# One sum, one inverse, one product a group: where the attention weights of batch 0 are divided

## The chip, the cores and the metric

The kernel runs on one core of a Trainium2 chip. The metric is device time in microseconds (us) of one execution. The core has five engines with programs of their own: TensorE (PE in the profile, with its weight loads as PEld), VectorE (DVE), ScalarE (ACT), GpSimd (POOL) and SyncE (SP, which here issues nearly all DMAs). Each engine runs its instructions in the order of its program and waits at semaphores for the others.

## The reference

Attention of 2 batches with 8 heads, 576 positions and 64 values a head, in which scores more than tau under the row's maximum are dropped; then two mixtures of dense layers over the 1152 tokens.

```
scores = scale * (q @ k^T)
scores = where(scores >= max(scores) - tau, scores, -1e9)
attn = exp(scores - max(scores))
attn = attn / (sum(attn) + 1e-9)
x = attn @ v                       # 1152 tokens x 512
h = max(x @ w1, x @ w2, x @ w3);  y = h @ w_out
out = sum over 4 experts e of p[:, e] * (relu(y @ m_w1[e]) @ m_w2[e])
```

## The kernel before

Every fp32 operand of a product is split in two parts of type fp32r, "hi" (the rounded value) and "lo" (the rest), and three or four products of parts make one. So nearly everything that TensorE reads was first copied once and subtracted once by ACT, DVE or POOL.

**Stages.** Stage A (`attention_fast`, L466) is the attention of batch 0 and has the core for itself. Stage B is the attention of batch 1, laid between the products of the dense layers of the first 512 tokens; then follow the dense layers of the other 640 tokens. The products (L832) can begin when stage A has delivered X, its result.

**Stage A.** Heads are taken in four pairs (jobs). A pair has two groups of queries and nine steps: a step is one tile of 128 queries of one head against 576 keys, and one step in nine holds the last 64 queries of both heads (`st.h is None`). A step runs through: `qk` (scores, PE, L301), `peak` (row maximum, DVE, L312), `power` (exp, ACT, L319), `limit` and `weigh` (DVE, L315 and L324: drops weights below the threshold and sums the row into `st_sum`), `norm` (L327), `turn` (transposes on PE, L342 and L345), `cut_hi` and `cut_lo` (split of the turned weights into `am`, for keys 0 to 511, and `ar`, for the last 64 keys). The big split goes by turns through PE and ACT (mode "pe") or through a copy `tcopy` and POOL (mode "pool"). When a group's steps are done, `gather` multiplies with the values (L418), adds the two halves of the product (L421 on ACT, L423 on DVE) and splits the sum into X (L432 on ACT, L435 on POOL).

`norm` divides the weights by their sum before they are turned: two instructions on one element a row on DVE, then a pass over 576 elements on POOL (on DVE for the last two steps):

```
nc.vector.tensor_scalar(out=su, in0=su, scalar1=1e-9, ..., op0=ALU.add)
nc.vector.reciprocal(out=re, in_=su)
last = (nc.vector if swift else nc.gpsimd).tensor_scalar(out=em, in0=em, scalar1=re, scalar2=even, op0=ALU.mult, op1=ALU.add)
```

`even` is 0 unless tau is negative; then all weights are dropped and every one becomes 1/576.

**Order.** In stage A the framework's scheduler orders each engine's instructions from the order in which the code issues them; from the dense layers on, the code's own order stands. In stage A step i is weighed while step i-1 is divided and turned and step i-2 is split. Buffers: scores, turned weights and all else in PSUM have two tiles each (`S`, `T`, `U`). Stage B calls the same `norm` and is otherwise not touched.

## Time and profile before

| what | before |
|---|---|
| time, median of 3 runs | 746.56 us (745.12 to 747.57) |
| the profiled execution's own time | 749.09 us |
| its span, first to last instruction | 747.3 us |
| PE, PEld busy over the span | 715.7, 636.4 us (96%, 85%) |
| DVE, ACT, POOL busy over the span | 378.3, 339.0, 392.4 us (51%, 45%, 53%) |
| mean granted TensorE clock | 0.988 |

The last 1.8 us of the own time lie around the span. A busy share over the whole span is a mean over stages that are limited by different things, so the rows below split the span.

### The profile page before, as it was taken

The page shows a single profiled execution, that of the slowest core. Times are in us where ns is not written, and L with a number is a line of the kernel's source. Part 1 is how long each engine was busy: PE and PEld are TensorE (multiplying, and loading weights), DVE is VectorE, ACT ScalarE, POOL GpSimd, SP SyncE. Part 2 cuts the span into 40 slices and gives each one's busy share as a digit, 9 for nine tenths or more (in the row PEclk, how much of TensorE's full clock was granted, in tenths as well). Part 3 has the DMA queues.
Part 4 walks back from the last instruction along what each step waited for, and adds up shares of the span by engine and source line. Part 5 has one row for each costly group of instructions (what it writes and reads, how often), then busy time and mean ns, then how long its engine had stood idle before and what let it go on. Part 6 is the DMA issues. An engine that isn't in the chain of part 4 may idle for free.

```text
span 747.3 us, 11716 instructions
## 1 busy us (share of the span) xinstructions
PE 715.7 (96%) x4103; PEld 636.4 (85%) x4103; DVE 378.3 (51%) x900; ACT 339.0 (45%) x716; POOL 392.4 (53%) x435
## 2 busy tenths in 40 slices
PE   4798999999899999999999999999999999999997
PEld 3787889777688788888888899999998998998996
DVE  6798988775265765766766421112222222222222
ACT  5688984444544655465454412333321321321320
POOL 5789785777554555564564524544623522522520
PEclk9799999999999999999999999999999999999999
DMA  6702006876724124122322233223412313312303
GB/s 183 227 22 49 1 1 187 261 226 204 199 78 113 59 73 122 57 73 57 86 61 66 71 113 85 68 58 91 132 50 85 99 43 85 104 45 77 113 2 71
DMA packets 89369, 71.01 MB, mean 95 GB/s; under 512 B 24158, under 2 KB 75358, under 8 KB 89310
## 3 DMA queue, kind: packets, MB, share of 16 engines
q1 hardware_dynamic: 88860, 69.96, 32.7%
q8 instruction: 33, 0.54, 0.3%
q10 hardware_dynamic: 418, 0.30, 0.2%
q14 instruction: 26, 0.21, 0.1%
q0 software_dynamic: 32, 0.00, 0.0%
HBM read 61.59 MB, written 8.65 MB: 94 GB/s over the span
## 4 chain that ended last, share of the span: by engine, by line
PE 77%; DVE 5%; ACT 5%; POOL 5%; issue 3%; DMA 3%; SPq 1%; POOLq 0%; ACTq 0%; DVEq 0%
PE ps L832 63%; PE u L418 5%; PE s L301 4%; PE t L342 3%; POOL a L630 2%; DVE st_negm L312 1%; DMA vrem<-in_v_dram 1%; ACT em L319 1%; DMA words<-in_moe_w_dram 1%; POOL b L656 1%; PE u L175 1%; DMA krem<-in_k_dram 1%; DVE raw L664 1%; ACT a L626 1%; PE t L388 1%
## 5 line engine op out<-in xcount | busy, mean ns | idle before, releaser
L630 POOL TENSOR_TENSOR a<-raw,a 128x512 fp32r<-128x512 f32 (+1 forms) x116 | 145.1, 1256 | 163.6 <-ACT a L626 160.3
L832 PE MATMUL ps<-b,hh 128*128 128x512 f32 x576 | 184.3, 393 | 0.0
L832 PEld LDWEIGHTS ps<-b,hh 128*128 128x128 f32 x576 | 107.3, 188 | 20.4
L782 ACT ACTIVATE hh<-ps 128x320 fp32r<-128x320 f32 (+1 forms) x96 | 46.8, 488 | 152.3 <-PE ps L832 151.9
L832 PE MATMUL ps<-b,hl 128*128 128x512 f32 x288 | 113.1, 393 | 0.0
L832 PE MATMUL ps<-y1h,a 128*128 128x320 f32 x512 | 112.8, 309 | 0.0
L630 POOL TENSOR_TENSOR b<-raw,b 128x512 fp32r<-128x512 f32 x64 | 82.8, 1296 | 53.4 <-ACT b L626 53.4
L785 DVE SCALAR_TENSOR_TENSOR hl<-ps,hh 128x320 fp32r<-128x320 f32 (+1 forms) x96 | 53.4, 556 | 108.9 <-ACT hh L782 108.8
L626 ACT ACTIVATE a<-raw 128x512 fp32r<-128x512 f32 (+1 forms) x116 | 69.4, 612 | 58.8 <-PE ps L832 19.1
L801 DVE SCALAR_TENSOR_TENSOR acc<-ps,pr,acc 128x512 f32<-128x512 f32 x63 | 47.2, 749 | 80.4 <-PE ps L832 80.3
L832 PE MATMUL ps<-y0h,a 128*128 128x512 f32 x256 | 85.1, 403 | 0.8 <-POOL a L630 0.8
L832 PEld LDWEIGHTS ps<-y1h,a 128*128 128x128 f32 x512 | 85.4, 188 | 0.3
L319 ACT ACTIVATE em<-s,st_negm 128x576 f32<-128x576 f32 x72 | 53.3, 744 | 70.9 <-DVE st_negm L312 70.7
L332 POOL TENSOR_SCALAR em<-em,st_r,even 128x576 f32<-128x576 f32 x70 | 57.5, 824 | 43.2 <-DVE st_r L331 41.6
L832 PE MATMUL ps<-y1l,a 128*128 128x320 f32 x256 | 79.1, 309 | 0.0
L312 DVE TENSOR_REDUCE st_negm<-s 128x1 f32<-128x576 f32 x72 | 54.1, 753 | 48.9 <-PE s L301 48.4
L301 PE MATMUL s<-K,QS 128*128 128x288 f32 x320 | 59.7, 315 | 6.4 <-DVE em L324 3.2
L832 PE MATMUL ps<-x1h,a 128*128 128x320 f32 x288 | 63.4, 309 | 0.0
L324 DVE SCALAR_TENSOR_TENSOR em<-s,st_thr,em 128x576 f32<-128x576 f32 x72 | 58.2, 812 | 9.9 <-ACT em L319 7.8
L832 PEld LDWEIGHTS ps<-b,hl 128*128 128x128 f32 x288 | 54.1, 188 | 10.0
L301 PEld LDWEIGHTS s<-K,QS 128*128 128x128 f32 x320 | 49.8, 197 | 11.3 <-issue 6.0
L832 PEld LDWEIGHTS ps<-y0h,a 128*128 128x128 f32 x256 | 47.8, 191 | 9.6 <-POOL a L630 1.2
(129 smaller groups left out, 1271.1 us busy)
## 6 DMA issues: line engine op xcount, KB each, us to landing
raw<-in_moe_w_dram SPq DMA_DIRECT2D x128, 256.0 KB
words<-in_moe_w_dram SPq DMA_DIRECT2D x18, 512.0 KB
kept_w<-raw SPq DMA_DIRECT2D x18, 256.0 KB
raw<-kept_w SPq DMA_DIRECT2D x18, 256.0 KB
kraw<-in_k_dram SPq DMA_DIRECT2D x30, 128.0 KB
words<-in_moe_w_out_dram SPq DMA_DIRECT2D x8, 384.0 KB
vraw<-in_v_dram SPq DMA_DIRECT2D x8, 256.0 KB
qraw<-in_q_dram SPq DMA_DIRECT2D x7, 256.0 KB
```

The costliest lines, as they stand in the source:

```text
L301: nc.tensor.matmul(st.s[:, kh, 0:HS], lhsT=l, rhs=r, start=i == 0, stop=i == len(terms) - 1)
L312: nc.vector.tensor_reduce(out=st.stat["negm"], in_=views(st)[0], op=ALU.max, axis=AX.XY, negate=True)
L319: nc.scalar.activation(out=ev, in_=sv, func=AF.Exp, bias=st.stat["negm"])
L324: nc.vector.scalar_tensor_tensor(out=ev, in0=sv, scalar=st.stat["thr"], in1=ev, op0=ALU.is_ge, op1=ALU.mult, accum_out=st.stat["sum"])
L332: last = (nc.vector if swift else nc.gpsimd).tensor_scalar(out=em, in0=em, scalar1=re, scalar2=even, op0=ALU.mult, op1=ALU.add)
L418: at["valued"] = nc.tensor.matmul(pv, lhsT=l, rhs=r, start=i == 0, stop=i == len(terms) - 1)
L626: nc.scalar.activation(out=b["hi"], in_=b["raw"], func=AF.Copy)
L630: nc.gpsimd.tensor_tensor(out=b["lo"], in0=b["raw"], in1=f32(b["hi"]), op=ALU.subtract)
L782: nc.scalar.activation(out=hs[f][0][:, a:z], in_=ps, func=AF.Relu)
L785: nc.vector.scalar_tensor_tensor(out=hs[f][1][:, a:z], in0=ps, scalar=0.0, in1=f32(hs[f][0][:, a:z]), op0=ALU.max, op1=ALU.subtract)
L801: nc.vector.scalar_tensor_tensor(out=accs[t], in0=ps, scalar=pe, in1=accs[t], op0=ALU.mult, op1=ALU.add)
L832: nc.tensor.matmul(ps, lhsT=l, rhs=r, start=i == 0, stop=i == count - 1)
```

## The change

For batch 0 the weights go undivided through the transposes, the split and the product with the values. `weigh` writes the sum of a step into its column of a tile `sums` of the group. When a group's last step is weighed, `invert` adds 1e-9 to the 4 or 5 sums and inverts them in one instruction each, and copies each over 64 columns into `inv`. In `gather` PE turns `inv` (2 or 3 transposes into a tile `rt`), so that the inverses stand along the queries as X does, and DVE multiplies X with them. Around this: a step is turned and split one step after it was weighed (before: split two steps after). The split of `ar` moves from DVE to POOL, by way of a copy `arcopy` that ACT makes. The copy of the values to "hi" moves from ACT to POOL. A negative tau is now handled by scores of 0 (`qscale` is 0 then, a scale read from a tile) in place of `even`.

```
 def weigh(st):
-    nc.vector.scalar_tensor_tensor(
+    return nc.vector.scalar_tensor_tensor(
         out=ev, in0=sv, scalar=st.stat["thr"], in1=ev, op0=ALU.is_ge, op1=ALU.mult, accum_out=st.stat["sum"])
-def norm(st, swift=False):
+def norm(st):
...
-    last = (nc.vector if swift else nc.gpsimd).tensor_scalar(out=em, in0=em, scalar1=re, scalar2=even, op0=ALU.mult, op1=ALU.add)
+    nc.gpsimd.tensor_scalar(out=em, in0=em, scalar1=re, scalar2=1.0, op0=ALU.mult, op1=ALU.mult)
+    twice(st)
...
+def invert(grp):
+    n = 5 if grp.n > grp.nn else 4
+    su = grp.sums[:, 0:n]
+    nc.vector.tensor_scalar(out=su, in0=su, scalar1=1e-9, scalar2=None, op0=ALU.add)
+    nc.vector.reciprocal(out=su, in_=su)
+    flats = grp.inv.rearrange("p c h d -> p (c h) d")
+    nc.vector.tensor_copy(out=flats[:, 0:4], in_=su[:, 0:4, None].to_broadcast([P, 4, D]))
+    if n == 5:
+        nc.vector.tensor_copy(out=flats[:, 4:6], in_=su[:, 4:5, None].to_broadcast([P, 2, D]))
...
 # values
-    nc.scalar.activation(out=V[:, :, :, 0:D], in_=vn, func=AF.Copy)
+    if job.b == 0:
+        nc.gpsimd.tensor_scalar(out=V[:, :, :, 0:D], in0=vn, scalar1=1.0, scalar2=1.0, op0=ALU.mult, op1=ALU.mult)
...
 # cut_hi
-        nc.scalar.activation(out=grp.ar[0][r, cols], in_=st.tm[r, r], func=AF.Copy)
+        if ar_pool:
+            if r.start == 0:
+                st.arcopy = atile([P, P], F32, "arcopy")
+            nc.scalar.activation(out=st.arcopy[r, r], in_=st.tm[r, r], func=AF.Copy)
...
 # cut_lo
-        nc.vector.tensor_tensor(out=grp.ar[1][r, cols], in0=st.tm[r, r], in1=f32(grp.ar[0][r, cols]), op=ALU.subtract)
+        if hasattr(st, "arcopy"):
+            hi, lo = (x[r, cols] for x in grp.ar)
+            nc.gpsimd.tensor_scalar(out=hi, in0=st.arcopy[r, r], scalar1=1.0, scalar2=1.0, op0=ALU.mult, op1=ALU.mult)
+            nc.gpsimd.tensor_tensor(out=lo, in0=st.arcopy[r, r], in1=f32(hi), op=ALU.subtract)
...
 # gather
+    if grp.job.b == 0:
+        rt = ptile_at("U", [P, 3 * P])
+        for x in range(3 if n > grp.nn else 2):
+            nc.tensor.transpose(rt[:, x * P:(x + 1) * P], grp.inv[:, x].rearrange("p h d -> p (h d)"), ident)
+        parts = [(slice(0, P), slice(0, grp.nn), slice(0, grp.nn))]
+        if n > grp.nn:
+            parts += [(slice(h * D, (h + 1) * D), slice(grp.nn, n), slice(grp.nn + h * REM, grp.nn + (h + 1) * REM)) for h in range(2)]
+        for r, c, rc in parts:
+            nc.vector.tensor_tensor(out=x32[r, c], in0=rt[r, rc], in1=x32[r, c], op=ALU.mult)
+        yield
...
 # attention_fast
-    for i in range(n + 3):
+    for i in range(n + 1):
-        old = steps[i - 2] if 0 <= i - 2 < n else None
+        old = steps[i - 1] if i else None
...
+            if st:
+                at["weighed"] = weigh(st)
+                twice(st)
+                if st.last:
+                    invert(st.grp)
...
-bufs_a = {"K1": 2, "K2": 2, "QS": 2, "V": 2, "VR": 2, "em": 3, "am": 6, "ar": 4}
+bufs_a = {"sums": 2, "inv": 1, "K1": 2, "K2": 2, "QS": 2, "V": 2, "VR": 2, "em": 3, "am": 6, "ar": 3}
```

The changed file has other line numbers; in it `qk` is L305, `peak` L322, `limit` L325, `power` L329, `weigh` L334, `invert` L355 to L360, `turn` L367 and L370, the copies of `ar` L407 to L433, the products with the values L453, the sum of halves L458, the turn of `inv` L464 and the new product L469.

On VectorE, in the middle of stage A, these ten instructions stood in a row (`st_sum` and `st_r` are a step's sum and its inverse, `u` the PSUM tile that holds the turned last keys):

```order
L324 SCALAR_TENSOR_TENSOR em,st_sum<-s,st_thr,em 128x576
L315 TENSOR_SCALAR st_thr<-st_negm,ntau 128x1
L400 TENSOR_TENSOR ar<-u,ar 128x128
L330 TENSOR_SCALAR st_sum<-st_sum 128x1
L331 RECIPROCAL st_r<-st_sum 128x1
L324 SCALAR_TENSOR_TENSOR em,st_sum<-s,st_thr,em 128x576
L312 TENSOR_REDUCE st_negm<-s 128x1
L330 TENSOR_SCALAR st_sum<-st_sum 128x1
L315 TENSOR_SCALAR st_thr<-st_negm,ntau 128x1
L331 RECIPROCAL st_r<-st_sum 128x1
```

and now, where a group ends (here the first pair's second group is inverted and its first group's result `x_407` is multiplied):

```order
L356 RECIPROCAL sums<-sums 128x5
L458 TENSOR_TENSOR x_407<-u,pvlo 64x256
L325 TENSOR_SCALAR st_thr<-st_negm,ntau 128x1
L334 SCALAR_TENSOR_TENSOR em,sums<-s,st_thr,em 128x576
L358 COPY inv<-sums 128x256
L360 COPY inv<-sums 128x128
L469 TENSOR_TENSOR x_407<-u,x_407 128x256
L334 SCALAR_TENSOR_TENSOR em,sums<-s,st_thr,em 128x576
L322 TENSOR_REDUCE st_negm<-s 128x1
L325 TENSOR_SCALAR st_thr<-st_negm,ntau 128x1
L322 TENSOR_REDUCE st_negm<-s 128x1
L334 SCALAR_TENSOR_TENSOR em,sums<-s,st_thr,em 128x576
```

The two small instructions of each step and the subtraction for `ar` have left; once a group an inverse, one or two copies and a product have come.

On TensorE, the first group's products with the values stood together, each head's product of `ar` right behind those of `am`:

```order
L342 MATMUL t<-ident,em 128x128 x4
L418 MATMUL u<-am,V 128x256 x4
L418 MATMUL u<-ar,VR 128x256
L418 MATMUL u<-am,V 128x256 x4
L418 MATMUL u<-ar,VR 128x256
L345 MATMUL u<-ident,em 128x128
```

and now the products of `ar`, whose operand comes from POOL, stand behind other work:

```order
L367 MATMUL t<-ident,em 128x128 x4
L453 MATMUL u<-am,V 128x256 x4
L305 MATMUL s<-K_132,QS 128x288
L305 MATMUL s<-K_133,QS 128x288
L305 MATMUL s<-K_132,QS 128x288
L305 MATMUL s<-K_133,QS 128x288
L176 MATMUL u<-ident,QN 128x128 x4
L418 MATMUL t<-ident,em 128x128 x4
L425 MATMUL t<-am,nident 128x512
L453 MATMUL u<-ar,VR 128x256
L453 MATMUL u<-am,V 128x256 x4
```

Between the first four products and the one of `ar` there are now 13 matmuls of other steps.

On ScalarE, at the start of stage A, four steps' exponentials (`em<-s`) stood ahead of the copies of pair 1's values (`V`, `VR`), which wait for DMAs; of them these two, from one row on:

```order
L319 ACTIVATE em<-s,st_negm 128x576 x2
L626 ACTIVATE a<-raw 128x512
L646 ACTIVATE b<-words 128x512
L246 ACTIVATE V<-vraw 128x8x64
L252 ACTIVATE VR<-vrem 64x64 x2
L319 ACTIVATE em<-s,st_negm 128x576
L375 ACTIVATE am<-t 128x4x128
```

and now three do, and the split of step 0 (`am`, `arcopy`) has come ahead of `VR`:

```order
L329 ACTIVATE em<-s,st_negm 128x576
L666 ACTIVATE a<-raw 128x512
L400 ACTIVATE am<-t 128x4x128
L407 ACTIVATE arcopy<-u 128x128
L666 ACTIVATE a<-raw 128x512
L686 ACTIVATE b<-words 128x512
L256 ACTIVATE VR<-vrem 64x64 x2
L426 ACTIVATE am<-t 128x4x128
L329 ACTIVATE em<-s,st_negm 128x576
```

The copy `V` has gone to POOL, and the fourth exponential stands behind `VR`. On SP the load of pair 1's values, `vraw`, has moved behind four of the five loads of `pr` and pair 2's `qraw`.

## Rows read from the trace of the kernel before

**Rows 1.** Windows: busy us and count per engine, then granted clock, DMA share, GB/s.

```profile
0.00:29.40 29.40, 15.31 (x61) 12.76 (x62) 18.80 (x53) 16.61 (x34) 16.74 (x32) 0.77 0.72 208
29.40:106.80 77.40, 72.12 (x542) 66.16 (x540) 70.38 (x233) 68.49 (x153) 66.82 (x95) 1.00 0.15 38
106.80:114.00 7.20, 6.55 (x47) 5.89 (x45) 5.87 (x16) 4.36 (x12) 3.18 (x5) 1.00 0.00 0
114.00:747.30 633.30, 621.67 (x3460) 551.61 (x3458) 283.23 (x601) 249.56 (x518) 305.66 (x305) 1.00 0.34 98
```

**Rows 2.** Groups by line and shape on DVE, 30 to 114 us: busy us, mean ns.

```profile
L324 DVE SCALAR_TENSOR_TENSOR em<-s,st_thr,em 128x576 f32<-128x576 f32 x31 | 24.9, 812 | 2.3 <-ACT em L319 1.5 <-issue 0.4
...
L331 DVE RECIPROCAL st_r<-st_sum 128x1 f32<-128x1 f32 x32 | 4.8, 155 | 0.3
L400 DVE TENSOR_TENSOR ar<-u,ar 128x128 fp32r<-128x128 f32 x16 | 4.4, 278 | 0.0
L330 DVE TENSOR_SCALAR st_sum<-st_sum 128x1 f32<-128x1 f32 x31 | 4.4, 146 | 0.3
...
L398 DVE TENSOR_TENSOR am<-t,am 128x256 fp32r<-128x256 f32 x8 | 3.1, 412 | 0.0
...
L400 DVE TENSOR_TENSOR ar<-u,ar 64x64 fp32r<-64x64 f32 x8 | 1.7, 219 | 0.1
```

**Rows 3.** Timeline of DVE: start us, duration us, instruction.

```profile
71.98 0.14 DVE L330 TENSOR_SCALAR st_sum<-st_sum 128x1 f32<-128x1 f32 x1
72.05 0.81 DVE L324 SCALAR_TENSOR_TENSOR em<-s,st_thr,em 128x576 f32<-128x576 f32 x1
...
74.50 0.28 DVE L400 TENSOR_TENSOR ar<-u,ar 128x128 fp32r<-128x128 f32 x1
74.70 0.75 DVE L312 TENSOR_REDUCE st_negm<-s 128x1 f32<-128x576 f32 x1
```

**Rows 4.** Groups by line and shape on POOL, 30 to 114 us.

```profile
L332 POOL TENSOR_SCALAR em<-em,st_r,even 128x576 f32<-128x576 f32 x31 | 25.4, 824 | 3.6 <-DVE st_r L331 2.2 <-DVE st_sum L330 0.7 <-PE u L175 0.4
...
L392 POOL TENSOR_SCALAR am<-tcopy 128x512 fp32r<-128x512 f32 x15 | 9.6, 637 | 2.8 <-ACT tcopy L372 2.7
L435 POOL TENSOR_TENSOR x0l<-x,x0h 128x256 fp32r<-128x256 f32 x7 | 5.1, 732 | 3.2 <-ACT x0h L432 3.1
...
L195 POOL TENSOR_SCALAR K<-K 128x64 fp32r<-128x64 f32 x6 | 1.4, 241 | 0.0
...
L435 POOL TENSOR_TENSOR x1l<-x,x1h 128x64 fp32r<-128x64 f32 x3 | 1.0, 320 | 0.0
```

**Rows 5.** Timeline of DVE at the start.

```profile
3.58 0.29 DVE L206 COPY kraw<-kraw 128x256 f32<-128x256 f32 x1 [0.29 <-DMA kraw<-in_k_dram]
...
5.11 0.15 DVE L898 TENSOR_SCALAR neg<-tau_c 128x1 f32<-128x1 f32 x1 [1.23 <-DMA tau_c<-in_tau_dram]
```

**Rows 6.** Timeline of PE: two runs of four transposes.

```profile
98.35 0.60 PE L342 MATMUL t<-ident,em 128*128 128x128 f32 x4
98.78 0.60 PE L388 MATMUL t<-ident,em 128*128 128x128 f32 x4
```

**Rows 7.** Waits of PE's weight loads, 30 to 114 us: total us, times, longest.

```profile
PEld u L418 <- DVE ar L400: 1.8, 2, 1.5
...
PEld t L342 <- POOL em L332: 0.9, 1, 0.9
```

**Rows 8.** Timeline at the end of stage A.

```profile
106.78 0.82 DVE L324 SCALAR_TENSOR_TENSOR em<-s,st_thr,em 128x576 f32<-128x576 f32 x1
...
108.47 0.58 DVE L332 TENSOR_SCALAR em<-em,st_r,even 128x576 f32<-128x576 f32 x1
...
110.40 0.60 PE L342 MATMUL t<-ident,em 128*128 128x128 f32 x4
```

**Rows 9.** Timeline of ACT at the start of stage A.

```profile
25.96 0.63 ACT L246 ACTIVATE V<-vraw 128x512 fp32r<-128x512 f32 x1 [1.55 <-DMA vraw<-in_v_dram]
...
27.56 0.74 ACT L319 ACTIVATE em<-s,st_negm 128x576 f32<-128x576 f32 x1
```

More of the change, by code (lines that the diff above doesn't have):

```diff
@@ L91, in fused_kernel @@
     nc.gpsimd.dma_start(out=tau_c, in_=tau.rearrange("(a o) -> a o", o=1).to_broadcast([P, 1]))
+    qscale = cst.tile([P, 1], F32, name="qscale")
     def xy_tiles(g, nm):
@@ L177, in prep @@
             qo = (0, W + 2 * REM)[h]
-            nc.scalar.activation(out=QS[:, qo:qo + MAIN], in_=tq, func=AF.Copy, scale=SCALE)
+            nc.scalar.activation(out=QS[:, qo:qo + MAIN], in_=tq, func=AF.Copy, scale=qscale)
             yield
@@ L189, in prep @@
             nc.scalar.activation(out=k1r, in_=trk, func=AF.Copy)
-            nc.scalar.activation(out=q1r, in_=trq, func=AF.Copy, scale=SCALE)
+            nc.scalar.activation(out=q1r, in_=trq, func=AF.Copy, scale=qscale)
             yield
@@ L219, in head @@
             nc.scalar.activation(out=d1, in_=tk, func=AF.Copy)
-            nc.scalar.activation(out=QS[:, qo:qo + MAIN], in_=tq, func=AF.Copy, scale=SCALE)
+            nc.scalar.activation(out=QS[:, qo:qo + MAIN], in_=tq, func=AF.Copy, scale=qscale)
             nc.vector.tensor_tensor(out=K2[:, ko:ko + MAIN], in0=tk, in1=f32(d1), op=ALU.subtract)
@@ L234, in prep_first @@
         head(1)
-        nc.scalar.activation(out=q1r, in_=trq, func=AF.Copy, scale=SCALE)
+        nc.scalar.activation(out=q1r, in_=trq, func=AF.Copy, scale=qscale)
         for t in (K1, K2):
@@ L245, in values @@
         vn = vt[:, :, :, 0, :]
-        nc.scalar.activation(out=V[:, :, :, 0:D], in_=vn, func=AF.Copy)
+        if job.b == 0:
+            nc.gpsimd.tensor_scalar(out=V[:, :, :, 0:D], in0=vn, scalar1=1.0, scalar2=1.0, op0=ALU.mult, op1=ALU.mult)
+        else:
+            nc.scalar.activation(out=V[:, :, :, 0:D], in_=vn, func=AF.Copy)
         nc.gpsimd.memset(f32(VR), 0.0)
@@ L310, in peak @@
         st.col = (st.h or 0) * S
-        st.stat = {x: atile([P, 1], F32, f"st_{x}") for x in ("negm", "thr", "sum", "r")}
+        st.stat = {x: atile([P, 1], F32, f"st_{x}") for x in ("negm", "thr", "sum", "r") if st.grp.job.b or x in ("negm", "thr")}
+        if not st.grp.job.b:
+            if not hasattr(st.grp, "sums"):
+                st.grp.sums, st.grp.inv = atile([P, 5], F32, "sums"), atile([P, 3, 2, D], F32, "inv")
+            col = 4 if st.h is None else 2 * st.ci + st.h
+            st.stat["sum"] = st.grp.sums[:, col:col + 1]
         nc.vector.tensor_reduce(out=st.stat["negm"], in_=views(st)[0], op=ALU.max, axis=AX.XY, negate=True)
@@ L378, in cut_hi @@
                 grp.ar = [atile([P, grp.n], F32R, "ar") for _ in "hl"]
-            nc.scalar.activation(out=grp.ar[0][r, cols], in_=st.tm[r, r], func=AF.Copy)
+            if ar_pool:
+                if r.start == 0:
+                    st.arcopy = atile([P, P], F32, "arcopy")
+                nc.scalar.activation(out=st.arcopy[r, r], in_=st.tm[r, r], func=AF.Copy)
+            else:
+                nc.scalar.activation(out=grp.ar[0][r, cols], in_=st.tm[r, r], func=AF.Copy)
     def cut_lo(st):
@@ L497, in attention_fast @@
                 peak(st)
-            if 0 <= i - 1 < n - 1:
-                norm(steps[i - 1], i - 1 >= n - SWIFT)
             if nxt:
@@ L504, in attention_fast @@
                 qk(nxt)
-            if st and not nxt:
-                power(st)
-                limit(st)
-                weigh(st)
-                at["normed"] = norm(st, True)
-                turn(steps[i - 1])
-                urgent.enter_context(tc.issue_after(at["normed"].ins))
             if old:
-                cut_hi(old, next(modes) if old.h is not None and i - 2 < n - CALM else "dve")
+                at["turned"] = turn(old)
             advance()
-            if nxt:
+            if st:
                 power(st)
             if old:
-                cut_lo(old)
-            if nxt:
+                cut_hi(old, next(modes) if old.h is not None and i - 1 < n - CALM else "dve", i - 1 < n - CALM)
+            if st:
                 limit(st)
             advance()
-            if nxt:
-                weigh(st)
-                if i:
-                    turn(steps[i - 1])
-            if st and not nxt:
-                at["turned"] = turn(st)
+            if old:
+                cut_lo(old)
+            if st:
+                at["weighed"] = weigh(st)
+                twice(st)
+                if st.last:
+                    invert(st.grp)
             if old:
@@ L895, in fused_kernel @@
     stage = open_attention("A", {"S": 2, "T": 2, "U": 2}, bufs_a)
-    neg = cst.tile([P, 1], F32, name="neg")
-    nc.vector.tensor_scalar(out=neg, in0=tau_c, scalar1=0.0, scalar2=None, op0=ALU.is_lt)
-    even = cst.tile([P, 1], F32, name="even")
-    nc.vector.tensor_scalar(out=even, in0=neg, scalar1=1.0 / S, scalar2=None, op0=ALU.mult)
+    nc.vector.tensor_scalar(out=qscale, in0=tau_c, scalar1=0.0, scalar2=SCALE, op0=ALU.is_ge, op1=ALU.mult)
     ntau = cst.tile([P, 1], F32, name="ntau")
-    nc.vector.scalar_tensor_tensor(out=ntau, in0=neg, scalar=3e38, in1=tau_c, op0=ALU.mult, op1=ALU.subtract)
+    nc.vector.tensor_scalar(out=ntau, in0=tau_c, scalar1=0.0, scalar2=-1.0, op0=ALU.max, op1=ALU.mult)
     for _ in attention_fast(first, cycle(MODES_A)):
```

11 lines of the change are left out of this document (7 added, 4 removed).

## The prediction

> **What bounds the kernel now.** I read the windows first, cut where the work changes [rows 1]. Behind 114 us stand the dense layers and batch 1's attention, and PE is busy for 621.67 of 633.30 us there: that part starts when stage A ends and takes what it takes. The change touches it in one place only, a constant in batch 1's division on POOL, which is at half load there. So what it is worth is read from the 114 us before. The first 29.4 us run at a mean granted clock of 0.77 (a part of them at 1.2 GHz) with the DMA engines 72% busy; they are ruled by what has landed. From 29.4 to 106.8 us the clock is 1.00 (2.4 GHz), the DMA share is 0.15, and the reader is to see that no engine is far behind another: PE 72.12 of 77.4 us (93%), its weight loads 66.16 (85%), DVE 70.38 (91%), ACT 68.49 (88%), POOL 66.82 (86%). In the last 7.2 us the tail runs out and PE begins to fill itself with products of the dense layers.
>
> Then the waits. PE's are few and short: of those in the list, 1.8 us fall to the split of `ar` on DVE and 0.9 us to the division on POOL [rows 7]. The exponentials are waited for by L324 for 1.5 us in all [rows 2]. With so little waiting, the length of the stage is mostly what the fullest engine has to do, so I count what each gets and loses. Which engine is the fullest is the first thing to choose: by matmul time it is PE, by weight loads it is DVE. Matmul durations overlap: two runs of four transposes are shown with 0.60 us each but start 0.43 us apart [rows 6], so PE can take more than its 93% seem to allow. I take DVE.
>
> The Trainium skill says the same in Perfetto Trace Analysis, Identifying the Most-Contended Engine: TensorE's matmul busy share is no good measure and its weight-load share is, while VectorE's occupancy may be taken as it stands. By that rule the bound is DVE, 91% against 85%, and the sum is the one below; by the matmul share it would be that of the first rival.
>
> **The change part by part.** The profiled execution took 749.09 us, 1.8 us more than its span and 2.5 us more than the median of 746.56; the sum is made against 749.09 and carried over to the median as a difference.
>
> DVE loses the two one-element instructions of 36 steps, 72 in all. Each lasts 0.146 or 0.155 us [rows 2], but the next instruction can start 0.07 us after one [rows 3]; they wait for each other, so I take 0.10, 7.2 us (5.0 to 11.2). It loses 15 of 16 subtractions for `ar` of 128x128 and 6 of 8 of 64x64 (the last group keeps DVE): 0.278 and 0.219 us long, the next instruction 0.20 us after the larger [rows 2, 3], so 15 x 0.20 + 6 x 0.17 = 4.0 us (to 5.5). Together 11.2 us (9 to 16.7).
>
> DVE gains, over 8 groups, 16 small instructions on the sums at 0.10: 1.6 us (1.1 to 2.5). Eight copies of a sum over 64 columns, 128x256, which no row shows: bounds are a one-element instruction, 0.15, and the 128x256 subtraction from PSUM, 0.412 [rows 2]; the nearest is the plain copy of 128x256 in SBUF at 0.29 [rows 5], which I take, 2.3 us (1.2 to 3.3). Four of 128x128, between 0.15 and 0.29: 0.20, 0.8 us (0.6 to 1.2). Eight products of 128x256 with one operand in PSUM: the subtraction of that size, 0.412 less the 0.08 by which such instructions overlap, 0.33: 2.7 us (to 3.3). Eight of 64x64 at 0.17: 1.4 us (to 1.75). Together 8.8 us (7 to 12). The last group's share, some 1.3 us, comes after the last step, where PE multiplies for the dense layers; if that cover were gone it would cost its 1.3 us. Each new product also makes DVE wait for the turned inverses, with the next step's maximum and threshold behind it: a wait that no row shows, between nothing and one run of transposes, 0.43 us [rows 6], a group; since the turn can be done a step ahead, I take nothing. So 7.5 us fall into the stage, and DVE is relieved by 3.7 us (bounds: 10 us relieved, 3 us burdened). As DVE is the bound for nine tenths of the time, **3.4 us**.
>
> POOL loses 34 divisions of 0.824 us, 28.0 us. It gains four copies of values, 4 x 0.637 = 2.5 us, and the split of `ar`: one pass between 0.241 (64 columns) and 0.637 (512), say 0.30, and one with two operands between 0.320 and 0.732, say 0.46 [rows 4]; 15 x 0.76, and 6 of 64x64 at 0.56 as the upper bound, 14.8 us. It is left with 10.7 us less. ACT loses the four copies, 4 x 0.63 [rows 9]. Neither is the bound, so both stand at nothing, but one hand-over from DVE to POOL to PE is gone from each step: PE's wait of 0.9 us for the division [rows 7] goes: **0.9 us**. What is late next in its place is the threshold's product itself, L324, which the transposes now wait for directly.
>
> PE gains 20 transposes (2 for each of four groups, 3 for the others) at 0.43 / 4 = 0.11 us [rows 6], 2.2 us, in an idle time of 5.3 us by matmuls and 11.2 by weight loads [rows 1]. From nothing to all 2.2; since PE is second to DVE by a little only, I take half: **+1.1 us**.
>
> The tail: after the last L324 the sum, the inverse and a division of 0.58 us on DVE stood before the last transposes, which began 110.40 - 107.60 = 2.8 us after its end [rows 8]. They can now begin at once. PE had products to do meanwhile, so what it can win is its idle time there, 7.20 - 6.55 = 0.65 us by matmuls and 1.31 by weight loads [rows 1]: **1.0 us**. The new product of the last group delays the last X by under 1 us, and the products that need it stand behind many that don't.
>
> The start: at 25.96 us ACT waited 1.55 us for `vraw`, and the fifth exponential came at 27.56 [rows 9]. The copy is POOL's now, but the other one, `VR`, has moved ahead of the fourth exponential, and `vraw` stands later on SP: behind the copy on POOL wait the split of `am` and `ar` of the first group. From nothing to one step, 77.4 / 31 = 2.5 us [rows 1, 2]; the earlier split of step 0 works against it, so **+0.6 us**. The scale read from a tile needs tau, which landed by 5.11 us [rows 5], before the first transposed queries were there: nothing.
>
> Sum: -3.4 - 0.9 + 1.1 - 1.0 + 0.6 = -3.6 us; 745.5 for the profiled execution, 743.0 us beside the median.
>
> **The rivals.** First: PE is the bound already, as its 93% says, and DVE's relief is worth nothing. Then PE's 2.2 us count in full: +2.2 - 0.9 - 1.0 + 0.6 = +0.9, **747.5 us**. For it speaks that PE's wait list is short; against it, that runs of transposes overlap [rows 6].
>
> Second, slower: the split of `ar` becomes what PE waits for. Each group's products end with it; before, one DVE instruction of 0.278 stood between ACT's copy and PE, now two passes on POOL of 0.76 together, and POOL may be in a copy of 0.637 or a subtraction of 0.732 [rows 4] when they become ready. `arcopy` is a single buffer, so ACT, with the next exponentials behind it, waits for POOL too. At 1.0 us for each of 8 groups the result is -3.6 + 8.0 = +4.4, **751.0 us**; it decides from 3.6 / 8 = 0.45 us a group on. For it: this hand-over was already PE's largest wait, 1.8 us in two [rows 7]. Against it: 13 matmuls of other steps now stand in between, and POOL has more room.
>
> Third, more than forecast: what held the stage were the hand-overs among four engines of nearly equal load, and with POOL at three quarters they close up until PE's weight loads are the floor: 66.16 + 2.0 = 68.2 of 77.4 us, -9.2; with half of that gained beyond the sum, **738.3 us**. Against it speaks that DVE would have to do what is left to it, 70.4 - 3.7 = 66.7 us, in 69.2 us almost without a gap.
>
> **How the numbers follow.** Forecast (739.1 to 744.3) 0.52, first rival 0.20, second 0.18, third 0.10. About 0.3%, 2.2 us, is what a measurement of this kernel can tell from no change. Faster: 0.52 + 0.10 = 0.62; same 0.20; slower 0.18. The range takes in the third rival for the most part and the second up to 0.8 us a group: 737.5 to 749.5 us; without the rivals it would be 739.1 to 744.3.
>
> **What would show it.** Stage A's last L334 (L324 before) should end near 105 us of the span (107.6 now, less 2.6 without the tail's 1.0) and the first dense products follow with the same spacing. DVE's busy time in the stretch should fall by 3 to 4 us with its share still at 90% or more; the broadcast copies should take about 0.29 us, the new products 0.41. PE's weight-load share should rise to 88% or so. I am wrong if the wait list shows PE or ACT on POOL's `ar` for more than 4 us in all, if the first steps end later than before by more than one step, or if the stretch stays as long while DVE's share falls to 85%.

## The result and the profile after

The changed kernel takes 757.53 us (median of 4 runs, 756.92 to 758.74) against 746.70 for the kernel before: a ratio of 1.0144 [1.0127, 1.0161], 10.8 us slower where 3.6 us less was forecast. The profiled execution took 757.06 us with a span of 755.3, 8.0 more than the span of 747.3 before. The profile of before is of an execution that took 749.09 us, 2.4 above its median, so the two profiles show 8.0 of the 10.8 us.

Where these 8.0 us lie is read from the first weighing that both kernels show in full swing (the fifth) and the last. The fifth starts at 28.56 us (before 28.34), the last at 112.69 (before 106.78, [rows 8]), the span ends 642.6 us later (before 640.5). So the start costs 0.2, the steady part 84.1 - 78.4 = 5.7, the tail 2.1. The 0.2 says little: over the profiles of all kernels below, the fifth weighing starts between 26.02 and 31.47 us. Here it is before (L324) and now (L334):

```profile
28.34 0.82 DVE L324 SCALAR_TENSOR_TENSOR em<-s,st_thr,em 128x576 f32<-128x576 f32 x1 [2.35 <-ACT em L319]
...
28.56 0.80 DVE L334 SCALAR_TENSOR_TENSOR em<-s,st_thr,em 128x576 f32<-128x576 f32 x1
```

Windows of the changed kernel, cut as in [rows 1]:

```profile
0.00:29.40 29.40, 16.66 (x84) 13.60 (x84) 19.51 (x48) 19.32 (x41) 17.41 (x36) 0.88 0.79 232
29.40:106.80 77.40, 68.59 (x499) 63.05 (x500) 64.13 (x170) 60.42 (x136) 52.02 (x95) 0.98 0.11 28
106.80:114.00 7.20, 5.10 (x40) 4.49 (x39) 6.00 (x16) 5.30 (x11) 4.39 (x9) 1.00 0.01 2
114.00:755.30 641.30, 630.02 (x3503) 556.62 (x3503) 288.17 (x617) 253.75 (x526) 304.47 (x309) 1.00 0.33 97
```

In the second row every engine has become less dense: PE 89% (93% before), DVE 83% (91%), ACT 78% (88%), POOL 67% (86%). Nothing has become the bound; all wait more. Cut at the fifth and the last weighing, so that both rows hold the same stretch of work, before and now:

```profile
28.34:106.78 78.44, 72.99 (x544) 66.59 (x542) 71.38 (x236) 69.09 (x155) 67.78 (x96) 0.99 0.15 40
...
28.56:112.69 84.13, 73.40 (x537) 67.33 (x536) 69.67 (x186) 65.34 (x145) 57.08 (x103) 0.98 0.11 28
```

DVE's busy time has fallen by 1.7 us and its share from 91% to 83%, while the stretch has become longer: this is one of the signs by which the prediction said it would be wrong.

What the engines wait for, the waits of PE's weight loads tell, 30 to 114 us (total us, times, longest), which answer to [rows 7]:

```profile
PEld s L305 <- DVE em L334: 5.0, 6, 1.6
PEld u L464 <- ACT arcopy L407: 2.1, 3, 1.1
PEld u L370 <- DVE x L469: 1.9, 2, 1.0
PEld u L370 <- DVE x L458: 1.4, 1, 1.4
...
PEld u L166 <- ACT arcopy L407: 1.0, 1, 1.0
PEld u L453 <- ACT arcopy L407: 1.0, 1, 1.0
...
PEld u L453 <- POOL ar L432: 0.6, 1, 0.6
```

Five of these seven rows are waits for a free `u`, a PSUM tile of kind U, together 7.4 us. In two of them, 4.0 us, the inverses take part: their turn (L464) waits until ACT has read the turned last keys, and the next turn of last keys (L370) until DVE has multiplied with the inverses (L469). In the other three, `u` is held by last keys or by a product with the values. The largest such row of before is this one:

```profile
PEld u L175 <- DVE K L171: 0.8, 2, 0.5
```

The largest gap between two weighings, 8.4 us, shows some of these waits, and more (timeline, a part of the rows):

```profile
64.80 0.38 ACT L456 ACTIVATE pvlo<-u 64x256 f32<-64x256 f32 x1
64.93 0.27 PE L370 MATMUL u<-ident,em 128*128 128x128 f32 x1
65.21 0.42 DVE L458 TENSOR_TENSOR x<-u,pvlo 64x256 f32<-64x256 f32 x1 [2.16 <-ACT pvlo L456]
65.24 0.28 ACT L407 ACTIVATE arcopy<-u 128x128 f32<-128x128 f32 x1
...
65.57 0.44 PE L464 MATMUL u<-ident,inv 128*128 128x128 f32 x2 [0.37 <-ACT arcopy L407]
...
66.34 0.41 DVE L469 TENSOR_TENSOR x<-u,x 128x256 f32<-128x256 f32 x1
...
66.67 0.70 DVE L358 COPY inv<-sums 128x256 f32<-128x256 f32 x1
66.81 0.33 PE L370 MATMUL u<-ident,em 128*128 128x128 f32 x1 [0.69 <-DVE x L469]
...
67.30 0.47 DVE L360 COPY inv<-sums 128x128 f32<-128x128 f32 x1
67.69 0.81 DVE L334 SCALAR_TENSOR_TENSOR em<-s,st_thr,em 128x576 f32<-128x576 f32 x1
...
68.56 1.29 PE L305 MATMUL s<-K,QS 128*128 128x288 f32 x4 [1.42 <-DVE em L334]
```

On DVE, the sum of halves waits 2.16 us; behind it stand, in the order of the program, the product with the inverses, then two copies for the next group, and only then the weighing. The last weighing before this one began at 59.32. In this gap the two waits for `u` (0.37 and 0.69 us) are the smaller part; the wait for ACT's `pvlo` is 2.16 us, and the product and the copies take 1.35 us ahead of the weighing (66.34 to 67.69). PE is idle for 1.42 us before the next scores, whose four matmuls take 1.29 us instead of 0.69.

The Trainium skill names such a thing in Perfetto Trace Analysis, Optimization Strategy: the same gap coming again on an engine that should be full can mean that SBUF or PSUM has no room for the next tile. Here the rows on `u` agree with it.

The last products of stage A, which began at 110.75 us before (first row; L418), begin at 117.91 (timeline, answering to [rows 8]):

```profile
110.75 0.83 PE L418 MATMUL u<-am,V 128*128 128x320 f32 x4
...
112.69 0.82 DVE L334 SCALAR_TENSOR_TENSOR em<-s,st_thr,em 128x576 f32<-128x576 f32 x1
...
114.17 0.60 PE L367 MATMUL t<-ident,em 128*128 128x128 f32 x4
...
117.91 0.82 PE L453 MATMUL u<-am,V 128*128 128x320 f32 x4 [0.72 <-DVE ar L435]
```

### The profile page after: what moved, and what is told of

Same layout as the page of the kernel before. It is cut to its first block, busy times and chain, and to the rows that moved or that the text cites. A ratio compares the mean times of both kernels' runs of the same rounds, so it can differ in the third digit from the quotient of the medians.

```text
span 755.3 us, 11678 instructions
## 1 busy us (share of the span) xinstructions
PE 720.4 (95%) x4123; PEld 637.8 (84%) x4123; DVE 377.8 (50%) x848; ACT 338.8 (45%) x712; POOL 378.3 (50%) x447
## 4 chain that ended last, share of the span: by engine, by line
PE 75%; DVE 4%; POOL 3%; issue 2%; ACT 1%; SPq 1%; DMA 0%; POOLq 0%; ACTq 0%; DVEq 0%
PE ps L872 64%; PE u L453 4%; PE s L305 3%; PE t L367 2%; POOL a L670 1%; POOL b L696 1%; DVE raw L704 1%; PE u L176 1%; ACT a L666 1%; DVE hmax L750 1%; POOL hl L758 1%; DVE st_negm L322 1%; SPq L130 0%; DMA vraw<-in_v_dram 0%; DVE bits L699 0%
## 5 line engine op out<-in xcount | busy, mean ns | idle before, releaser
L329 ACT ACTIVATE em<-s,st_negm 128x576 f32<-128x576 f32 x72 | 53.2, 742 | 71.7 <-DVE st_negm L322 71.5
L322 DVE TENSOR_REDUCE st_negm<-s 128x1 f32<-128x576 f32 x72 | 54.2, 755 | 53.1 <-PE s L305 52.7
L305 PE MATMUL s<-K,QS 128*128 128x288 f32 x320 | 58.7, 310 | 8.3 <-DVE em L334 7.8
L334 DVE SCALAR_TENSOR_TENSOR em<-s,st_thr,em 128x576 f32<-128x576 f32 x72 | 58.4, 813 | 12.4 <-ACT em L329 10.2
L305 PEld LDWEIGHTS s<-K,QS 128*128 128x128 f32 x320 | 49.6, 195 | 14.5 <-DVE em L334 7.2
L872 PE MATMUL ps<-y0l,a 128*128 128x512 f32 x128 | 51.2, 400 | 0.4 <-ACT a L666 0.4
```

The costliest lines, as they stand in the source:

```text
L305: nc.tensor.matmul(st.s[:, kh, 0:HS], lhsT=l, rhs=r, start=i == 0, stop=i == len(terms) - 1)
L322: nc.vector.tensor_reduce(out=st.stat["negm"], in_=views(st)[0], op=ALU.max, axis=AX.XY, negate=True)
L329: nc.scalar.activation(out=ev, in_=sv, func=AF.Exp, bias=st.stat["negm"])
L334: return nc.vector.scalar_tensor_tensor(out=ev, in0=sv, scalar=st.stat["thr"], in1=ev, op0=ALU.is_ge, op1=ALU.mult, accum_out=st.stat["sum"])
L872: nc.tensor.matmul(ps, lhsT=l, rhs=r, start=i == 0, stop=i == count - 1)
```

## The experiments

All medians are in us; each ratio is to the kernel before in the same series. "Weighings" is the time from the start of the fifth to that of the last, "tail" from there to the end of the span, both of the profiled execution.

| kernel | median | ratio, 95% | weighings | tail |
|---|---|---|---|---|
| before | 746.0 to 747.7 | | 78.4 | 640.5 |
| changed | 757.53 | 1.0144 [1.0127, 1.0161] | 84.1 | 642.6 |
| e1 | 755.99 | 1.0103 [1.0067, 1.0138] | 80.7 | 641.5 |
| e2 | 756.57 | 1.0120 [1.0095, 1.0146] | 84.5 | 642.8 |
| e3 | 752.46 | 1.0065 [1.0045, 1.0084] | 77.8 | 640.6 |
| e4 | 754.72 | 1.0099 [1.0079, 1.0120] | 79.0 | 646.0 |
| e5 | 750.36 | 1.0043 [1.0024, 1.0061] | 77.8 | 643.3 |
| e6 | 746.74 | 0.9992 [0.9975, 1.0009] | 75.4 | 639.7 |
| e7 | 759.43 | 1.0160 [1.0136, 1.0183] | 85.3 | 645.0 |
| e8 | 753.29 | 1.0083 [1.0061, 1.0105] | 81.4 | 640.5 |
| e9 | 754.93 | 1.0109 [1.0081, 1.0137] | 84.8 | 640.4 |
| e10 | 757.62 | 1.0142 [1.0122, 1.0161] | 82.3 | 646.0 |
| e11 | 750.61 | 1.0046 [1.0027, 1.0065] | 75.7 | 644.3 |
| e12 | 753.12 | 1.0074 [1.0046, 1.0101] | 81.6 | 643.4 |
| e13 | 749.29 | 1.0038 [1.0018, 1.0058] | 81.3 | 639.8 |
| e14 | 755.06 | 1.0121 [1.0102, 1.0140] | 84.8 | 640.6 |
| e15 | 754.32 | 1.0111 [1.0091, 1.0132] | 83.8 | 641.3 |
| e16 | 747.67 | 1.0016 [1.0004, 1.0028] | 75.2 | 641.9 |
| e17 | 752.15 | 1.0073 [1.0055, 1.0092] | 80.3 | 641.7 |
| e18 | 750.28 | 1.0036 [1.0018, 1.0053] | 77.6 | 640.3 |

Executions of one kernel lie up to 6 us apart (e12: 750.31 to 756.27), so a profile's parts need not add up to the median.

**e1, the old distance.** The changed kernel, with a step split two steps after its weighing as before; the copies into `inv` moved from `invert` to the start of the group's inverse path in `gather`.

```
-        for i in range(n + 1):
-            old = steps[i - 1] if i else None
+        for i in range(n + 2):
+            old = steps[i - 2] if i > 1 else None
```

> The changed kernel with the old depth of the pipeline: a step is split two steps after it was weighed, and turned after the weighing of the next step, as before; undivided weights, the split of ar and the copy of the values on POOL stay. The copies of the inverses over 64 columns stand in the gather, since one tile must serve two groups. Theory D (the depth: each engine now waits for fresh results of the step just weighed): 745 to 749 us, and ACT's wait for the turned weights falls from 8.7 us to under 3. Theory M (the moves to POOL, whose results come late and hold PSUM tiles): 756 to 759 us, nothing gained. Theory G (the group's inverse: one more PSUM tile of two, and a burst on DVE in front of the weighing): 754 to 758 us.

1.5 us less, the weighings 3.4 us shorter, but they start later, at 31.47. The 745 to 749 us of theory D did not come; the time lies in theory G's range and at the edge of theory M's.

**e2, the moves undone.** The changed kernel, but `ar` split on DVE and V copied on ACT.

```
-        if job.b == 0:
+        if job.b == 9:
             nc.gpsimd.tensor_scalar(out=V[:, :, :, 0:D], in0=vn, ...)
-                cut_hi(old, next(modes) ..., i - 1 < n - CALM)
+                cut_hi(old, next(modes) ...)
```

> The changed kernel with the split of ar back on DVE and the copy of the values back on ACT; all else as changed. Theory D: 755 to 759 us, no better than the changed kernel, since the depth stays. Theory M: 744 to 749 us. Theory G: 755 to 758 us; waits of PE's loads for arcopy (4 us) vanish, those for the product L469 and the sum L458 stay.

1.0 us less, which can't be told from nothing, and theory M's 744 to 749 us did not come: the moves are not what makes the changed kernel slow.

**e3, no division.** The changed kernel without `invert` and without the inverses in `gather`.

```
-                if st.last:
-                    invert(st.grp)
-        if grp.job.b == 0:
+        if grp.job.b == 9:
             rt = ptile_at("U", [P, 3 * P])
```

> The changed kernel without any division in batch 0: no inverse, no copies, no transposes of inverses, no product; the output of batch 0 leaves the division by the sum out. Theory D: the moved work saves its own time only, 753 to 757 us. Theory M: 754 to 757 us. Theory G: 744 to 749 us, and the gaps of 7 to 8 us between two weighings at the end of a pair's first group shrink to 4.

With no division at all the weighings last 77.8 us (78.4 before), and the median is still 4.8 us above before, outside the ranges of all three theories; the two largest gaps between weighings are 6.50 and 6.25 us, not 4. So of the 10.8 us some 4.8 are there without any inverse, and 5.1 come with it, each with the order that it drew.

**e4, undivided weights in the old order.** e1 and e2 together, with four buffers of `ar` as before.

> Of the change only the undivided weights, the group's inverse and the product with the result, in the old pipeline (split two steps after the weighing), with the split of ar on DVE, the copy of the values on ACT and four tiles for ar, as before. Theory D: 742 to 747 us, the forecast without the moves. Theory M: the same, 742 to 747 us. Theory G: 752 to 757 us.

As theory G said. The weighings are about as long as before (79.0 for 78.4); the tail is 5.5 us longer. Its timeline on PE and DVE (L467 turns the inverses, L472 is the product, L450 the values):

```profile
112.06 0.44 PE L467 MATMUL u<-ident,inv 128*128 128x128 f32 x2 [1.29 <-DVE x L455]
...
113.25 0.42 DVE L472 TENSOR_TENSOR x<-u,x 128x256 f32<-128x256 f32 x1
113.73 1.44 PE L450 MATMUL u<-am,V 128*128 128x320 f32 x4 [0.79 <-DVE x L472]
```

The inverses wait for a U tile that a product with the values holds, and the next product with the values waits until DVE has read the inverses. That led to the next edit.

**e5 and e8, the inverses in a tile of kind T,** e5 in e4, e8 in the changed kernel.

```
-            rt = ptile_at("U", [P, 3 * P])
+            rt = ptile_at("T", [P, 3 * P])
```

> This is the kernel of e4 (weights undivided, inverted by group, split two steps after the weighing as before, ar's split on DVE, the copy of the values on ACT) with one edit: the turned inverses rt take a PSUM tile of kind T, not of kind U. Theory U (the inverse path costs because it needs a third U tile per group while there are two, held by the products of the two heads): the last group's products start near 111 us of the span (113.7 in e4, 110.8 before), the span after the last weighing falls from 646.0 to 641-643 us, time 750 us. Theory B (what costs is the row of instructions on DVE at a group's end, whatever tile the transposes go to): the tail stays near 646, time 754-755 us.

> The changed kernel with one edit: rt takes a PSUM tile of kind T, not U. Theory U: the gaps of 8.4 and 7.3 us between weighings at the second and third pair's end close to 5 us or less, 28.56 to last weighing falls from 84.1 to 79-80 us, time 752-753 us. Theory B: as the changed kernel, 756.5-758.5 us, gaps of over 7 us stay.

Both fall as theory U said, by 4.4 and 4.2 us, and theory B's times did not come. Not all of theory U's numbers held: e8's weighings take 81.4 us (79 to 80 forecast), and its largest gaps at the two pairs' ends are 5.9 and 5.7 us (5 or less). e5's last products begin at 109.39 us (113.73 in e4), by its timeline of PE:

```profile
107.25 0.38 PE L467 MATMUL t<-ident,inv 128*128 128x128 f32 x2
...
109.39 0.84 PE L450 MATMUL u<-am,V 128*128 128x320 f32 x4 [0.25 <-ACT am L397]
```

In e8 the waits of PE's weight loads that answer to the 7.4 us of the changed kernel come to 0.5 us. Those behind the product with the inverses are now waits for T, 1.5 us; all rows of the list together fall less, from 15.6 to 13.4 us:

```profile
PEld s L305 <- DVE em L334: 3.3, 5, 1.0
...
PEld t L418 <- DVE x L469: 0.9, 1, 0.9
...
PEld t L367 <- DVE x L469: 0.6, 1, 0.6
```

**e6, no division in the old order** (e4 without sums inverted, copied, turned or multiplied).

> The kernel of e4 without any division in batch 0: no addition, inverse, copies, transposes of inverses or product (the output leaves the division out). It prices the inverse path in the old order, and tests the bound that the prediction chose. If DVE is the bound of stage A (the prediction): DVE loses 7.2 us (72 small instructions at 0.10) and keeps the split of ar, so the last weighing starts near 100 us of the span, time near 740 us. If the length comes from hand-overs in the order of the program, not from a full engine: last weighing near 106 us as before (e3, which has the shallow order and the moves: 106.7), span after it 640-641, time 745-748 us. Theory U or B for e4: e6 is 5-8 us under e4's 754.7 us.

No change that can be told. With DVE as the bound it would have come near 740 us, its last weighing near 100; that starts at 104.29. The window from 29.4 to 104 us, of before and of e6:

```profile
29.40:104.00 74.60, 69.32 (x521) 63.69 (x520) 67.65 (x222) 66.11 (x148) 64.78 (x93) 1.00 0.15 39
...
29.40:104.00 74.60, 69.63 (x525) 64.59 (x525) 65.64 (x173) 67.05 (x149) 42.21 (x63) 1.00 0.14 36
```

POOL is at 57% and DVE at 88% (87% and 91% before), and by the medians nothing is won. In the profiles e6's weighings are shorter, 75.4 for 78.4 us, but the execution profiled lies 0.9 us under its median, that of before 1.7 above the median of this series. And e6 has an order of its own: this run shows what the relief was worth here, not in every order.

**e7, the moves alone,** in the kernel before.

> The kernel before with the two moves alone: the split of ar on POOL by way of arcopy, and the copy of batch 0's values on POOL; division by step, order and buffers as before. Theory M (the moves cost): POOL, 86% busy before, gets 17 us more work and becomes what the division and PE wait for: last weighing 3 us or more later, time 750 us or above. Rival (moves cost nothing by themselves): 746.5-748.5 us, last weighing near 107 us.

12 us slower. The same window of e7:

```profile
29.40:104.00 74.60, 64.43 (x461) 56.53 (x460) 59.30 (x186) 59.07 (x134) 71.79 (x123) 1.00 0.13 33
```

POOL is at 96%, with almost no gap left: here one engine is likely the bound, as theory M said.

**e9, e8 with the moves undone.**

> The changed kernel with rt in a PSUM tile of kind T (as e8) and with the two moves undone (as e2: the split of ar on DVE, the copy of the values on ACT). The loss of the changed kernel is 10.8 us; e8 took 4.2 of it, e2 alone 1.0. If the tile and the moves are two hand-overs of which each hides the other (theory U with M): e9 gains more than the 5.2 us of both, 747-750 us, first to last weighing of steps 5 to 36 in 78-79 us. If the moves are harmless here: 752-753.5 us, as e8; what is left then belongs to the shorter distance between weighing and split (theory D).

1.6 us above e8, outside what either view gave: theory U with M fell. The intervals of e8 and e9 overlap.

**e10, more of the big split on POOL** (e5 with one edit).

```
-    MODES_A = ("pe", "pool")
+    MODES_A = ("pe", "pool", "pool")
```

> The kernel of e5 with one edit: of three big splits two go through POOL and one through PE (before by turns). It asks whether the room that the division leaves on POOL (54% busy in e5's stretch, 86% before) is worth something. Some five splits change sides: PE loses about 0.8 us each (four transposes and a product, 0.43 and 0.39 us of path), ACT one copy of 0.60 each, POOL gains 1.9 each, 9.5 us in all, to some 67%. If PE and ACT set the length (they are the fullest with DVE): 4 us less than e5, 746-747 us, no slower than before. If the order of hand-overs sets it: 749-752 us, as e5; a slower turn if PE waits for POOL's split of 1.9 us instead of ACT's of 0.6.

7.3 us slower than e5. The same window of e10:

```profile
29.40:104.00 74.60, 66.23 (x462) 59.20 (x460) 66.77 (x185) 58.32 (x129) 45.80 (x65) 0.95 0.12 29
```

PE and ACT had less to do, POOL is at 61%, and no engine but DVE (90%) is near its share of before: relieving PE was of no use in the order that came with it. A part of PE's work ran at 1.2 GHz, as the mean clock of 0.95 shows (1.00 in e5's window).

**e11, e1 with the inverses in T.**

> The kernel of e1 (the changed one with the split two steps after the weighing and the copies of the inverses in the gather; both moves kept) with rt in a tile of kind T. Against e5 it differs by the moves alone (and by ar's 3 buffers in place of 4). Theory M: what was slow in e7 was POOL at 96%; with the division gone POOL has room, so the moves cost under 1.5 us: 750-752 us. Rival: the two passes on POOL behind ACT's copy are waited for whatever POOL's load: 753-756 us, PE or ACT waiting for ar or arcopy for more than 3 us in all.

As e5: with the division gone POOL carries the moves at no cost that can be told.

**e12, the inverses not turned** (e5; the product reads `inv` itself).

```
-            rt = ptile_at("T", [P, 3 * P])
-            for x in range(3 if n > grp.nn else 2):
-                nc.tensor.transpose(rt[:, x * P:(x + 1) * P], ...)
+            rt = grp.inv.rearrange("p c h d -> p (c h d)")
```

> The kernel of e5 with the inverses not turned: the product of DVE takes the untransposed tile inv instead of rt, in the same shapes (so the weights are divided by the sums of wrong queries). PE loses the 20 transposes and no PSUM tile is taken; DVE keeps its sums, inverses, copies and products. e5 is 3.6 us over e6, which has no division at all. If that is DVE's added work of some 8 us (DVE 94% busy in e5): 749.5-750.5 us, as e5. If it is the transposes and their tile on PE's way: 746.5-747.5 us, as e6. Between them: both, in shares.

Neither: with 20 transposes less it is 2.8 us slower by the medians, though the two intervals overlap. Compared place by place without line numbers (`t` and `u` taken as one), 98 of the first 198 rows of DVE's timeline differ from e5's, and only 11 of e5's have no counterpart. So this edit had also drawn a new order, and the question became what an order alone is worth.

**e13 to e18, other orders of the same work.** e13 is the kernel before, e15 the changed one, e16 and e17 e11, e18 e5, with the next pair prepared later; e14 is the kernel before with the turns of the big split exchanged.

```
-    LOAD_A, PREP_A, LOAD_B, PREP_B = 0, 1, 1, 3
+    LOAD_A, PREP_A, LOAD_B, PREP_B = 0, 2, 1, 3
```

(`PREP_A` is 3 in e17), and in e14

```
-    MODES_A = ("pe", "pool")
+    MODES_A = ("pool", "pe")
```

> The kernel before with the preparation of the next pair's queries and keys issued one step later (PREP_A 2 in place of 1): the same work, another order of the engines' programs, since the framework's scheduler orders stage A. Theory S (the time of stage A hangs on the order that the scheduler happens to give, and the kernel before has a good one): 3 us or more slower, 750-757 us, with no engine doing more. Theory R (the losses of the changed kernel belong to its tile, depth and moves, and order alone is worth little): 745.5-749 us.

> The kernel before with the turns of the big split the other way round: the first step's goes through POOL, the second's through PE, and so on (before: PE first). As many of each kind within one. Theory S: 3 us or more slower, 750-757 us. Theory R: 745.5-749 us.

> The changed kernel with the preparation of the next pair issued one step later (PREP_A 2), the same work in another order. Theory S: it moves by 3 us or more either way from 757.5 us; if it falls to 752 us or below, most of the loss was order. Theory R: 756-759 us.

> The kernel of e11 (the change with the split two steps after the weighing, rt in a tile of kind T, the moves kept; 750.6 us) with the preparation of the next pair issued one step later. Theory S: it moves by 3 us or more either way, and can come out under the kernel before, 747 us. Theory R: 749.5-751.5 us.

> The kernel of e11 and e16 with the preparation of the next pair issued one step later still (PREP_A 3). Theory S: another draw of the order; e11 gave 750.6, e16 747.7 us, so 744-753 us, and under 746 us if the division by group can win anything in a good order. Theory R (the later preparation is better for its own sake): 745-747.5 us.

> The kernel of e5 (as e16, but ar's split on DVE and the copy of the values on ACT; 750.4 us) with PREP_A 2. Theory S: 746-755 us, and which of e16 and e18 is ahead says nothing of the moves. Theory R (the later preparation takes 3 us off kernels that divide by group: e15 from the changed kernel, e16 from e11): 746.5-748.5 us.

The kernel before becomes 3.3 and 9.1 us slower, the changed one 3.2 us faster, e11 2.9 faster and 1.5 slower, e5 stays. By the ratios, which leave the series out, e15, e16 and e17 move by -2.5, -2.2 and +2.0 us, and in each pair the intervals still overlap a little. So theory S is shown by e13 and, far beyond any noise, by e14, while e13's 749.29 and e16's 2.9 lie just under what it asked for; that the later preparation is better for its own sake fell with e13 and e17. e14's row, against that of before at e6:

```profile
29.40:104.00 74.60, 64.40 (x472) 57.93 (x473) 62.47 (x208) 60.87 (x136) 60.27 (x85) 1.00 0.12 32
```

With the work of the kernel before, all five columns are lower (PE 86%, DVE 84%, POOL 81%), as in the changed kernel. From the fifth to the last weighing DVE is busy for 71.99 us in e14 and 71.38 before, but in 84.8 and 78.4 us.

**What the pairs say.** The edits draw new orders as well: by the comparison made for e12, e8 differs from the changed kernel in 118 of 198 rows, and e14, which changes nothing but the turns, from before in 124. An edit can be told from the draw of an order only when it has one sign in several kernels. The pairs, in us by the medians and, since some pairs lie in two series, by the ratios too:

| edit | pairs | by medians | by ratios |
|---|---|---|---|
| inverses from U to T | changed to e8, e4 to e5, e1 to e11, e2 to e9 | -4.2, -4.4, -5.4, -1.6, mean -3.9 | -4.6, -4.2, -4.3, -0.8, mean -3.5 |
| short distance back to the old one | changed to e1, e8 to e11, e2 to e4, e9 to e5 | -1.5, -2.7, -1.9, -4.6, mean -2.7 | -3.1, -2.8, -1.6, -4.9, mean -3.1 |
| the moves, division not on POOL | e2 to changed, e9 to e8, e4 to e1, e5 to e11, e18 to e16 | +1.0, -1.6, +1.3, +0.2, -2.6 | +1.8, -1.9, +0.3, +0.2, -1.5 |

The tile has one sign in four of four, though the last of the four is not clear of noise. The distance has, too; its edit also moves the copies of the inverses and, in e4 and e5, adds a fourth buffer of `ar`. The moves have no sign: nothing. The three lines are not independent of each other, since nearly all pairs are of the same eight kernels, in which each of the three edits is in or out.

Taken in a row from the changed kernel, the tile (to e8) gives back 4.2 us, the rest of the inverse path (to e3) 0.8, distance and moves together (to e6) 5.7: with that the 10.8 us are gone. On the other way the shares differ, and by what wait the shorter distance costs is not shown. What is left by that way, 3.6 us from e6 to e5, is the inverse path itself or its order: e3 to e8 adds 0.8 for it, and e12, with less of the path, was slower. That stays open.

## Why the prediction was wrong

**The bound.** The step that failed is "with so little waiting, the length of the stage is mostly what the fullest engine has to do", and with it "I take DVE". By the weight loads the waiting was not so little: the prediction named 2.7 us of the list behind [rows 7], and the 18 rows of that list come to 10.9 us (15.6 us in the changed kernel). e6 takes from DVE the 7.2 us of small instructions that the sum counted, from POOL the division, adds nothing, and stays within 0.3%. Nor was DVE's 91% a ceiling. In the same window DVE is busy for 71.27 us in e18, 67.65 in the kernel before (its row is at e6), and e18 takes 3.5 us more than that:

```profile
29.40:104.00 74.60, 69.95 (x535) 65.30 (x534) 71.27 (x196) 63.98 (x146) 41.39 (x62) 1.00 0.13 31
```

That is 96%. And e14 does the work of before at 84%, since its order fits less well. By the Trainium skill's rule (Perfetto Trace Analysis, Identifying the Most-Contended Engine) DVE was the engine to optimize first; e6, at 0.9992 [0.9975, 1.0009], does not bear that out here. The term of -3.4 us brought nothing: what the prediction wanted from DVE came in e6 twice over, for at most 1.9 us by that interval. Whether e6's order hides a gain is not shown, since e6 was not run in another. The first rival's half of it, that DVE's relief is worth nothing, fits; that PE is the bound instead isn't shown: e10 took work from PE and lost, in another order and at a lower clock.

**What was priced at nothing.** "Since the turn can be done a step ahead, I take nothing" was the second error: the turn needs a PSUM tile, and the two of kind U are taken by the products with the values and the turned last keys. Some 3.9 us by the pairs; in the trace, 7.4 us of waits for `u`, in 4.0 of which the inverses take part. The bound that the text gave, 0.43 us a group or 3.4 us, came from the length of the transposes and not from what holds the tile. The shorter distance between weighing and split had no term at all except at the start and in the tail: some 2.7 us by the pairs, by a way that stays open. And the 8.8 us of new work on DVE were set against what left it as if it didn't matter where they stand: the timeline above shows them in a row ahead of a weighing.

**Order.** Nothing in the sum or in the range allowed for the order that the scheduler draws, 3.3 and 9.1 us without any change of work. For the second alone the range, 737.5 to 749.5, would have had to reach 755.6.

**The other terms.** PE's wait for the division (-0.9) went, and waits for `u` came. The transposes (+1.1) are small beside their tile. The tail (-1.0) became +2.1: the transposes do begin 114.17 - 113.51 = 0.7 us after the last weighing's end (2.8 before), but its products end later. The start (+0.6) was 0.2. The products (0.417 and 0.216 for 0.41 and 0.22) and POOL's passes (0.298 and 0.478 for 0.30 and 0.46) were sized right; the copies (0.402 and 0.346 for 0.29 and 0.20) and the addition to five sums (0.281 for 0.15) were not, in part for the reason below.

**The second rival** had the sign and, with 1.0 us a group, 751.0 us; its mechanism isn't what happened. PE waited 0.6 us for POOL's `ar`, ACT 2.0, less than the 4 us that it asked for, and undoing the moves gains nothing that keeps its sign once the division is off POOL. What the rival did see is that `arcopy` holds things up: PE waited 4.1 us in three rows for ACT to copy the last keys out of `u`. In e7, with the division on POOL, the moves cost 12 us, in the order that they drew. **The third rival** was wrong: hand-overs opened.

No version is faster than the kernel before. e16 comes nearest, at 1.0016 [1.0004, 1.0028]; with no division at all e6 is 0.7 us under its series' median (between 1.9 under and 0.7 above), so dividing by group can't win much here in an order like those that were tried.

## What to carry to other kernels

When four engines are all near 90% and each runs its program in order, a busy share tells as much of how well the order fits as of what bounds the kernel: before counting relief as gain, take the work out whole (here the division) and see what the time does. A new intermediate result needs a tile as well as time: look what holds each tile of its kind, and for how long, before its wait is set to nothing. Where a scheduler draws the order, time two or three orders of the same work first; a change smaller than their spread has to show its sign in several of them.

## What was not expected of the hardware

**DVE behind POOL.** Copies on DVE from SBUF to SBUF took from 0.28 to 0.70 us in one shape, and additions on 128x5 from 0.16 to 0.57. Three of them in the changed kernel's timeline of DVE:

```profile
41.24 0.29 DVE L358 COPY inv<-sums 128x256 f32<-128x256 f32 x1
...
61.32 0.57 DVE L355 TENSOR_SCALAR sums<-sums 128x5 f32<-128x5 f32 x1
...
66.67 0.70 DVE L358 COPY inv<-sums 128x256 f32<-128x256 f32 x1
```

And POOL's timeline around the last two:

```profile
60.57 1.29 POOL L423 TENSOR_TENSOR am<-tcopy,am 128x512 fp32r<-128x512 f32 x1
...
65.96 1.27 POOL L423 TENSOR_TENSOR am<-tcopy,am 128x512 fp32r<-128x512 f32 x1
```

The addition ends at 61.89, POOL's subtraction at 61.86; the copy at 67.37, POOL's subtraction at 67.23. No instruction of POOL is under way at 41.24. The Trainium skill has it in SBUF — State Buffer, SBUF: two separate sides: VectorE, in a mode that uses two ports or with two inputs in SBUF, and GpSimd share a pair of ports that one of them holds for a whole instruction. The ends of these two pairs agree; which mode an instruction ran in, no run here shows. Not every instruction is held: an inverse of five sums ran its usual 0.18 us in the middle of a subtraction on POOL:

```profile
39.33 1.27 POOL L423 TENSOR_TENSOR am<-tcopy,am 128x512 fp32r<-128x512 f32 x1
...
39.72 0.18 DVE L356 RECIPROCAL sums<-sums 128x5 f32<-128x5 f32 x1
```

**The clock after a gap.** In the changed kernel PE was busy for 0.44 us from 66 to 68.5 us, and then ran at 1.2 GHz until some 72 us. Its windows there, with the granted clock third from the end:

```profile
66.00:68.50 2.50, 0.44 (x3) 0.14 (x1) 2.50 (x7) 1.63 (x5) 2.50 (x4) 1.00 0.00 0
68.50:70.00 1.50, 1.44 (x6) 1.42 (x7) 1.06 (x5) 0.00 (x0) 0.95 (x4) 0.54 0.06 11
70.00:72.00 2.00, 2.00 (x11) 2.00 (x10) 0.86 (x2) 1.26 (x3) 0.00 (x0) 0.50 0.00 0
```

A gap among hand-overs is so paid for again afterwards: the run of four transposes, 0.60 us elsewhere, took 1.06. In e4's tail, too, four products behind a wait took 1.44 us (granted clock 0.50 from 113.7 to 115.2 us), 0.84 in e5's (1.00).
